# Softmax sums inverted to rows by VectorE blocks and GpSimd transfers, in place of TensorE transposes

## The chip, the core and the metric

The kernel runs on one core of a Trainium2 chip. TensorE multiplies matrices, VectorE and ScalarE work on tiles in SBUF and PSUM, GpSimd and SyncE issue transfers. What counts is the device time of one run, in microseconds (us).

## The reference

Three stages in one launch, on 4 batches of 576 positions, all in float32:

```python
q_rot, k_rot = (rotate(q), rotate(k))                # 4 batches, 8 heads, 576 positions, width 64
scores = scale * np.matmul(q_rot, k_rot.transpose(0, 1, 3, 2))
attn = np.exp(scores - np.max(scores, axis=-1, keepdims=True))
attn = attn / (np.sum(attn, axis=-1, keepdims=True) + 1e-09)
x = heads_side_by_side(np.matmul(attn, v))           # (4, 576, 512)

xn = (x - mu) / np.sqrt(var + 1e-06) * g_ln          # first MLP, 512 -> 2048 -> 512
x = x + np.maximum(xn @ w_ch1, 0.0) @ w_ch2

h = gelu(x @ w_in)                                   # gated MLP with a mix over the positions
u, v = (h[..., :512], h[..., 512:])
v_s = w_sg @ ((v - mu) / np.sqrt(var + 1e-06) * g_ln) + b_sg[:, None]
out = x + (u * v_s) @ w_out
```

## The kernel before

Everything is kept with the channels on the partitions and the positions along the columns. The batches are four groups, 0 to 3. In a group the attention is cut into eight blocks: four pairs of heads, each with a full block (`hi` 0, 384 queries) and a half block (`hi` 1, 192 queries). A block runs through these steps:

- `unit`: TensorE makes the scores of 128 queries and both heads (tiles S, L299); VectorE takes the negated maximum of a row (L327), ScalarE the exponential (L336), which also adds up each row's sum in `su`, with the queries on the partitions.
- `turn` and `evac`: TensorE transposes the exponentials in 64-wide pieces into the PSUM tile T (L371); ScalarE or VectorE copies them out (L395 to L406).
- `scale`: VectorE adds 1e-9, inverts (L421) and spreads the inverse over 64 columns for each head (`rb`, L425 to L429).
- `values`: TensorE multiplies by the values (PV, L454), then transposes `rb` (L465), so that the inverse lies along the columns. ScalarE copies PV to `x0` (L467); VectorE multiplies `x0` by the transposed inverse from PSUM (L473, L477). In all blocks but the four full ones of group 0, PV and the inverse are the two banks of the one PSUM tile T, which `turn` uses too, and T is given back after the multiplication. In the four early blocks both stand in banks of the MLP.

The first MLP follows a group by one: LayerNorm (`ln`, `rest`), then passes of `up` (L728 to L730) and `down` (L758 to L760) matmuls, three for each tile since values are split in a high and a low part. Their results leave PSUM over ScalarE and VectorE (L736, L738). The weights are split by `convert` (L58, L60, L62, L708, L710) during the first part of the run. The gated MLP of all batches closes the program.

The order on every engine is fixed when the program is built. `Sched` holds tasks as generators; each step names its engine, the earliest time and a planned duration, and the step that can start first on the planner's clock is written next, or one of lower rank that could start a little later. The ranks stand in tables (UNIT, RANK, TURN and others, by group). An engine then runs its own list strictly in that order, so a step that waits holds all that stands behind it on its engine. TensorE matmuls of `ones` (L562) fill planned gaps at the start. `x0` lives in a ring of XB = 9 tiles; the scores of a block wait until its tile is free.

Of the kernel before, what the change touches and what calls it, by code (L numbers as in the profile page):

```python
# [16 lines left out]
QB, KB, PB, TB, XB = 3, 4, 2, 2, 9  # L17
# [9 lines left out]
UNIT = [1.75, 2, 2.75, 4]  # L27
EVEN = [1, 0, 0, 3]
RANK = dict(end=-1, convert=2.75, prep=2.25, load=2, loader=2.75)
NORM, REST = [0.25, 2.75, 4.5, 2.5], [2.25, 2, 2.75, 4.5]  # L30
TURN, EVAC, VAL = [-1, 2.5, 3.5, 4], [1.5, 1.5, 1.5, 2.5], [2, 1.25, -1, 1.75]
# [116 lines left out]
class Attn:  # L148
# [10 lines left out]
    def __init__(self, tc, ctx, k, groups, sched):  # L159
# [6 lines left out]
        self.P, self.PT, self.QD = Bank(PB), Bank(TB), Bank(2)  # L166
        self.vin = [self.p.tile([128, 5, 128], F32, tag=f"vin{i}", name=f"vin{i}", bufs=1) for i in range(2)]
        self.qd = [self.p.tile([128, 128], F32, tag=f"qd{i}", name=f"qd{i}", bufs=1) for i in range(2)]
# [114 lines left out]
    def unit(self, i, heads=None):  # L283
# [18 lines left out]
        if heads[0] == 0:  # L302
            if u["t"] == 0:
                self.k["x0"](*x0)
                self.ahead(B["n"])
                B["su"] = self.p.tile([128, 6], F32, tag="su", name="su", bufs=3)
                B["left"] = 0
                B["turned"] = False
            u["P"], u["at"] = [], []
            u["nb"] = self.p.tile([128, 2], F32, tag="nb", name="nb", bufs=3)  # L310
# [103 lines left out]
    def scale(self, B, at):  # L414
# [7 lines left out]
        e = yield "DVE", 0.0, 0.4  # L422
        rb = B["rb"] = self.p.tile([128, 6, 64], F32, tag="rb", name="rb", bufs=2)
        if B["hi"]:
            nc.vector.tensor_copy(rb[:, 0:2, :], su[:, 0:2].unsqueeze(2).to_broadcast([128, 2, 64]))  # L425
            e = yield "DVE", 0.0, 0.2
            nc.vector.tensor_copy(rb[:, 2:4, :].rearrange("p a b -> p (a b)"), su[:, 2:3].to_broadcast([128, 128]))
        else:
            nc.vector.tensor_copy(rb, su.unsqueeze(2).to_broadcast([128, 6, 64]))  # L429
        B["inv"] = e + 0.1  # L430

    def values(self, B):
# [7 lines left out]
        for s, chs in enumerate(((0,), (1,), (2,), (3,), (4,)) if (B["g"], B["hi"]) in ALONE else ((0, 1, 2), (3, 4))):  # L440
            e = yield "PEc", (lambda: latest(B["ready"] if B["left"] == 0 else None, free(), V["v"])) if s == 0 else 0.0, 0.00168 * n * len(chs)
            self.pv = True
            if s == 0:
# [3 lines left out]
                else:  # L447
                    self.T.take()
                    both = self.ps.tile([128, 2, 512], F32, tag="T", name="PV")
                    ps, pb = both[:, 0, :], both[:, 1, :]  # L450
# [9 lines left out]
        f = yield "PE", lambda: latest(B.get("inv"), free() if early else 0.0), 0.08 + 0.00087 * n  # L460
        if early:
            bank2 = self.k["mpsb"].take()
            pb = self.k["mps"].tile([128, 512], F32, tag="m", name="inv")
        for i in range(3 if B["hi"] == 0 else 2):
            nc.tensor.transpose(pb[:, 128 * i:128 * i + 128], B["rb"][:, 2 * i:2 * i + 2, :].rearrange("p a b -> p (a b)"), self.k["ident"])  # L465
        e = yield "ACT", at + 0.35, 0.13 + 0.001 * n
        nc.scalar.copy(x0[:, q], ps[:, 0:n])  # L467
        if early:
            self.k["mpsb"].give(bank, e + 0.1)
        m = n if B["hi"] == 0 else 128  # L470
        e = yield "DVE", max(e, f + 0.25) + 0.1, 0.15 + 0.00105 * m
        a = q.start
        nc.vector.tensor_tensor(x0[:, a:a + m], x0[:, a:a + m], pb[:, 0:m], ALU.mult)  # L473
        for j in range(2) if B["hi"] else ():
            r = slice(64 * j, 64 * j + 64)
            e = yield "DVE", 0.0, 0.22
            nc.vector.tensor_tensor(x0[r, 512:576], x0[r, 512:576], pb[r, 128 + 64 * j:192 + 64 * j], ALU.mult)  # L477
        if early:
            self.k["mpsb"].give(bank2, e + 0.1)
        else:  # L480
            self.T.give(0, e + 0.1)
        n = B["ln"]
        self.rem[n] -= 1
        if self.rem[n] == 0:
            self.done[n] = e + 0.1
# [17 lines left out]
def fused_kernel(ctx, tc, q, k, v, cs, cst, w12, wi, wo, wsg, wsg4, gb, out):  # L503
# [39 lines left out]
    attn = Attn(tc, attn_ctx, dict(q=q, k=k, v=v, cs=csb, ident=ident, x0=get_x0, x0_free=x0_free, mps=mps, mpsb=mpsb), groups, C)  # L543
# [317 lines left out]
    for t in attn.qd:  # L861
# [341 lines left out]
```

## Time and profile before

| | |
|---|---|
| median of 3 runs | 932.64 us (931.2 to 932.87) |
| the profiled execution | 931.69 us, span 929.9 us |
| TensorE busy | 915.3 us, 98% of the span |
| VectorE, ScalarE busy | 600.4 us (65%), 495.2 us (53%) |
| GpSimd busy | 0.8 us, 9 instructions |
| mean granted TensorE clock | 0.998 |

The chain of work that ended last is 93% TensorE. Busy time of TensorE counts a pipelined matmul from its start to a modelled end, so what one costs is read from the start of one to the start of the next.

### The profile page before, as it was taken

How to read it: one execution, taken by the hardware profiler on the slowest of the kernel's cores; microseconds unless marked ns; L12 is line 12 of the kernel's file. 1: busy time of each engine (PE TensorE's matmuls, PEld its weight loads, DVE VectorE, ACT ScalarE, POOL GpSimd, SP SyncE). 2: the span in 40 equal slices, each digit the busy share in tenths (PEclk: the TensorE clock that was granted, in tenths of full speed). 3: DMA queues.
4: the chain of work that ended last, by engine and by line, in shares of the span. 5: the costliest groups of instructions: out<-in, count | busy, mean ns of one | idle time of the engine just before them, and what ended most of it. 6: DMA issues, size and time to landing. Idle time of an engine off the chain costs nothing.

```text
span 929.9 us, 18119 instructions
## 1 busy us (share of the span) xinstructions
PE 915.3 (98%) x7306; PEld 801.6 (86%) x7306; DVE 600.4 (65%) x1284; ACT 495.2 (53%) x1122; POOL 0.8 (0%) x9
## 2 busy tenths in 40 slices
PE   9998999999999999999999999999999999999998
PEld 9656778877988788779877799999999999999998
DVE  6868778888787645456764324663435897677654
ACT  3898888778365455463455513454313646373530
POOL 0000000000000000000000000000000000000000
PEclk9999999999999999999999999999999999999999
DMA  8366536676343363407633243988661201202011
GB/s 300 120 215 216 171 110 228 226 268 227 134 157 119 105 199 114 139 19 237 199 99 115 92 136 116 340 273 270 229 188 56 72 1 44 71 1 90 1 51 51
DMA packets 58067, 134.77 MB, mean 145 GB/s; under 512 B 8064, under 2 KB 30720, under 8 KB 57984
## 3 DMA queue, kind: packets, MB, share of 16 engines
q1 hardware_dynamic: 57152, 132.96, 43.2%
q8 instruction: 57, 0.93, 0.4%
q10 hardware_dynamic: 832, 0.66, 0.2%
q14 instruction: 26, 0.21, 0.1%
HBM read 106.50 MB, written 26.21 MB: 143 GB/s over the span
## 4 chain that ended last, share of the span: by engine, by line
PE 93%; DVE 3%; ACT 2%; issue 1%; POOL 0%; DVEq 0%; POOLq 0%
PE PV L454 9%; PE S L299 9%; PE m L758 8%; PE m L728 8%; PE m L759 7%; PE m L760 7%; PE m L730 7%; PE m L729 7%; PE T L371 5%; PE m L562 2%; PE p L1036 2%; PE p L1034 2%; PE p L1035 2%; PE p L1133 2%; PE p L1134 2%; PE p L1118 2%
## 5 line engine op out<-in xcount | busy, mean ns | idle before, releaser
L728 PE MATMUL m<-xh,w 128*128 128x288 f32 x480 | 148.0, 308 | 2.4 <-DVE h L738 2.4
L758 PE MATMUL m<-h,w 128*128 128x288 f32 x480 | 146.3, 305 | 0.0
L759 PE MATMUL m<-h,w 128*128 128x288 f32 x480 | 141.9, 296 | 0.0
L729 PE MATMUL m<-xl,w 128*128 128x288 f32 x480 | 141.6, 295 | 0.0
L730 PE MATMUL m<-xh,w 128*128 128x288 f32 x480 | 141.2, 294 | 0.0
L760 PE MATMUL m<-h,w 128*128 128x288 f32 x480 | 140.3, 292 | 0.0
L327 DVE TENSOR_REDUCE nb<-S 128x1 f32<-128x576 f32 x144 | 105.0, 753 | 35.0 <-PE S L299 30.5
L336 ACT ACTIVATE P<-S,nb 128x576 f32<-128x576 f32 x144 | 106.7, 744 | 36.1 <-DVE nb L327 35.3
L738 DVE SCALAR_TENSOR_TENSOR h<-m,h 128x288 fp32r<-128x288 f32 x128 | 58.3, 455 | 92.8 <-ACT h L736 91.5
L395 ACT COPY PT<-T 128x1024 f32<-128x1024 f32 (+6 forms) x118 | 75.0, 654 | 79.5 <-PE T L371 78.9
L736 ACT ACTIVATE h<-m 128x288 fp32r<-128x288 f32 x128 | 52.5, 410 | 92.5 <-PE m L730 91.1
L728 PEld LDWEIGHTS m<-xh,w 128*128 128x128 f32 x480 | 90.0, 187 | 9.4 <-DVE h L738 4.2
L299 PE MATMUL S<-K,qin 64*128 64x288 f32 x512 | 93.0, 430 | 1.7 <-ACT P L336 1.7
L758 PEld LDWEIGHTS m<-h,w 128*128 128x128 f32 x480 | 89.9, 187 | 5.4 <-issue 2.3
L759 PEld LDWEIGHTS m<-h,w 128*128 128x128 f32 x480 | 90.3, 188 | 0.5
L729 PEld LDWEIGHTS m<-xl,w 128*128 128x128 f32 x480 | 90.2, 188 | 0.6
L730 PEld LDWEIGHTS m<-xh,w 128*128 128x128 f32 x480 | 90.3, 188 | 0.0
L760 PEld LDWEIGHTS m<-h,w 128*128 128x128 f32 x480 | 90.2, 188 | 0.0
L454 PE MATMUL PV<-PT,vin 128*64 128x384 f32 (+1 forms) x640 | 87.3, 417 | 1.2 <-ACT PT L406 1.2
L371 PEld LDWEIGHTS T<-ident,P 64*128 64x128 f32 x1312 | 54.3, 138 | 29.3 <-DVE x L473 6.6
L454 PEld LDWEIGHTS PV<-PT,vin 128*64 128x64 f32 x640 | 43.8, 139 | 33.1 <-issue 27.2
L371 PE MATMUL T<-ident,P 64*128 64x64 f32 x1312 | 63.2, 227 | 4.7 <-DVE xc L587 1.9
(152 smaller groups left out, 1774.6 us busy)
## 6 DMA issues: line engine op xcount, KB each, us to landing
w<-wsc SPq DMA_DIRECT2D x96, 512.0 KB, 3.8
cd<-in_w SPq DMA_DIRECT2D x32, 512.0 KB, 4.5
wsc<-w SPq DMA_DIRECT2D x24, 512.0 KB, 3.6
kin<-in_k SPq DMA_DIRECT2D x15, 576.0 KB, 5.8
vin<-in_v SPq DMA_DIRECT2D x20, 320.0 KB, 3.7
qin<-in_q SPq DMA_DIRECT2D x15, 384.0 KB, 5.5
x1d<-x SPq DMA_DIRECT2D x32, 144.0 KB, 2.9
x<-x1d SPq DMA_DIRECT2D x32, 144.0 KB, 3.0
```

The source lines that it names most:

```text
L299: nc.tensor.matmul(S[j][:, n, :], q, Kb["K"][r, a:a + HQ], start=True, stop=True)
L327: nc.vector.tensor_reduce(nb[:, j:j + 1], S[j], AX.XY, ALU.max, negate=True)
L336: nc.scalar.activation(P[:, 576 * j:576 * j + 576].rearrange("p (n k) -> p n k", n=2), S[j], AF.Exp, bias=nb[:, j:j + 1], scale=1.0, accum ...
L371: nc.tensor.transpose(ps[:, j, 64 * n:64 * n + 64], x["tile"][r, 128 * i:128 * i + 128], self.k["ident"][r, r])
L395: copy(t[:, i:i + n, q0:q0 + 128].rearrange("p c (j q) -> p j c q", j=2), ps[:, :, 64 * s:64 * s + 64 * n].rearrange("p j (c q) -> p j c q ...
L454: nc.tensor.matmul(ps[r, 0:n], V["vin"][:, ch, r], t[:, 4 if ch == 4 else 5 * j + ch, 0:n], start=ch == 0, stop=ch == 4)
L728: nc.tensor.matmul(ps, w[:, 0, ms], xh[:, kc, :], start=kc == 0, stop=False)
L729: nc.tensor.matmul(ps, w[:, 0, ms], xl[:, kc, :], start=False, stop=False)
L730: nc.tensor.matmul(ps, w[:, 1, ms], xh[:, kc, :], start=False, stop=kc == 3)
L758: nc.tensor.matmul(ps, w[:, 0, ms], t[:, 0, :], start=a == 0, stop=False)
L759: nc.tensor.matmul(ps, w[:, 1, ms], t[:, 0, :], start=False, stop=False)
L760: nc.tensor.matmul(ps, w[:, 0, ms], t[:, 1, :], start=False, stop=a == n - 1)
```

## The change

In all blocks but the four full ones of group 0 (`ALONE`), the inverse sums no longer go through TensorE. `su` becomes a 128x32 tile that is set to zero once. VectorE transposes it in 32x32 blocks (`st`). GpSimd writes it with four small transfers to DRAM as rows of 128 queries (`inv`), and reads it back with two transfers (full block) or four (half block), each spread over 64 partitions, into `rb`, a 128x384 tile in SBUF. VectorE multiplies `x0` by `rb` in one instruction; T is given back after ScalarE's copy. `rb` has two buffers with a bank of their own in the planner (`R`). XB goes from 9 to 8, and all rank tables have other numbers, so that the order of the whole program is another one.

```diff
@@ -14,7 +14,7 @@
 DRAM = bass.MemoryType.DRAM
 
 HQ = 288
-QB, KB, PB, TB, XB = 3, 4, 2, 2, 9
+QB, KB, PB, TB, XB = 3, 4, 2, 2, 8
 WB, WX, CB = 8, 3, 4
 KC = (0, 288, 576)
 PARTS = (((0, 128), (128, 128), (256, 128)), ((384, 128), (512, 64)))
@@ -24,11 +24,11 @@
 HOLD = 0.3
 SWITCH = 0.3
 ALONE = ((0, 0),)
-UNIT = [1.75, 2, 2.75, 4]
...
-RANK = dict(end=-1, convert=2.75, prep=2.25, load=2, loader=2.75)
...
+UNIT = [1.75, 3, 1.75, 4]
...
+RANK = dict(end=0, convert=4.5, prep=4.5, load=4, loader=0.25)
...
 FG = [4, 8, 8, 4]
 
 AHEAD = 2
@@ -163,8 +163,9 @@
         self.S = [self.ps.tile([128, 2, 512], F32, tag=f"S{j}", name=f"S{j}")[:, :, 0:HQ] for j in range(2)]
         self.Sfree = [0.0, 0.0]
         self.T, self.qin, self.kin, self.vfree, self.K = Bank(), Bank(QB), Bank(2), Bank(2), Bank(KB)
-        self.P, self.PT, self.QD = Bank(PB), Bank(TB), Bank(2)
+        self.P, self.PT, self.QD, self.R = Bank(PB), Bank(TB), Bank(2), Bank(2)
         self.vin = [self.p.tile([128, 5, 128], F32, tag=f"vin{i}", name=f"vin{i}", bufs=1) for i in range(2)]
+        self.su = [self.p.tile([128, 32], F32, tag=f"su{i}", name=f"su{i}", bufs=1) for i in range(3)]
         self.qd = [self.p.tile([128, 128], F32, tag=f"qd{i}", name=f"qd{i}", bufs=1) for i in range(2)]
         self.done, self.rem, self.pv = {}, {}, False
         self.blocks, self.units = [], []
@@ -303,7 +304,7 @@
             if u["t"] == 0:
                 self.k["x0"](*x0)
                 self.ahead(B["n"])
-                B["su"] = self.p.tile([128, 6], F32, tag="su", name="su", bufs=3)
+                B["su"] = self.su[B["n"] % 3]
                 B["left"] = 0
                 B["turned"] = False
             u["P"], u["at"] = [], []
@@ -419,15 +420,33 @@
         nc.vector.tensor_scalar_add(su, su, 1e-9)
         e = yield "DVE", 0.0, 0.15
         nc.vector.reciprocal(su, su)
-        e = yield "DVE", 0.0, 0.4
-        rb = B["rb"] = self.p.tile([128, 6, 64], F32, tag="rb", name="rb", bufs=2)
-        if B["hi"]:
-            nc.vector.tensor_copy(rb[:, 0:2, :], su[:, 0:2].unsqueeze(2).to_broadcast([128, 2, 64]))
-            e = yield "DVE", 0.0, 0.2
-            nc.vector.tensor_copy(rb[:, 2:4, :].rearrange("p a b -> p (a b)"), su[:, 2:3].to_broadcast([128, 128]))
-        else:
-            nc.vector.tensor_copy(rb, su.unsqueeze(2).to_broadcast([128, 6, 64]))
-        B["inv"] = e + 0.1
+        if (B["g"], B["hi"]) in ALONE:
+            e = yield "DVE", self.R.free, 0.4
+            B["rslot"] = self.R.take()
+            rb = B["rb"] = self.p.tile([128, 384], F32, tag="rb", name="rb", bufs=2)
+            nc.vector.tensor_copy(rb.rearrange("p (a b) -> p a b", b=64), su.unsqueeze(2).to_broadcast([128, 6, 64]))
+            B["inv"] = e + 0.1
+            return
+        e = yield "DVE", 0.0, 0.2
+        st = self.p.tile([128, 32], F32, tag="st", name="st", bufs=2)
+        nc.vector.transpose(out=st, in_=B["su"])
+        D = self.k["dram"].tile([6, 128], F32, tag="inv", name="inv", bufs=4)
+        e = yield "POOL", e + 0.1, 4.4
+        for i in range(4):
+            nc.gpsimd.dma_start(out=D[0:k, 32 * i:32 * i + 32], in_=st[32 * i:32 * i + k])
+        for j in range(2):
+            e = yield "POOL", (lambda: latest(e + 3.0, self.R.free())) if j == 0 else 0.0, 2.2 if B["hi"] else 1.1
+            if j == 0:
+                B["rslot"] = self.R.take()
+                rb = B["rb"] = self.p.tile([128, 384], F32, tag="rb", name="rb", bufs=2)
+            r = slice(64 * j, 64 * j + 64)
+            if B["hi"]:
+                nc.gpsimd.dma_start(out=rb[r, 0:128], in_=D[j:j + 1].to_broadcast([64, 128]))
+                nc.gpsimd.dma_start(out=rb[r, 128:192], in_=D[2:3, r].to_broadcast([64, 64]))
+            else:
+                nc.gpsimd.dma_start(out=rb[r].rearrange("p (t q) -> p t q", q=128),
+                                    in_=D.rearrange("(t j) q -> j t q", j=2)[j:j + 1].to_broadcast([64, 3, 128]))
+        B["inv"] = e + 4.0
 
     def values(self, B):
 
@@ -447,7 +466,7 @@
                 else:
                     self.T.take()
                     both = self.ps.tile([128, 2, 512], F32, tag="T", name="PV")
-                    ps, pb = both[:, 0, :], both[:, 1, :]
+                    ps = both[:, 0, :]
             for ch in chs:
                 for j in range(2):
                     r = slice(64 * j, 64 * j + 64)
@@ -457,32 +476,34 @@
         if V["users"] == 0:
             self.vfree.give(V["vslot"], e)
         at = e
-        f = yield "PE", lambda: latest(B.get("inv"), free() if early else 0.0), 0.08 + 0.00087 * n
-        if early:
-            bank2 = self.k["mpsb"].take()
-            pb = self.k["mps"].tile([128, 512], F32, tag="m", name="inv")
-        for i in range(3 if B["hi"] == 0 else 2):
-            nc.tensor.transpose(pb[:, 128 * i:128 * i + 128], B["rb"][:, 2 * i:2 * i + 2, :].rearrange("p a b -> p (a b)"), self.k["ident"])
+        if not early:
+            e = yield "ACT", at + 0.35, 0.13 + 0.001 * n
+            nc.scalar.copy(x0[:, q], ps[:, 0:n])
+            self.T.give(0, e + 0.1)
+            e = yield "DVE", lambda: latest(e + 0.1, B.get("inv")), 0.15 + 0.00105 * n
+            nc.vector.tensor_tensor(x0[:, q], x0[:, q], B["rb"][:, 0:n], ALU.mult)
+            self.through(B, e + 0.1)
+            return
+        f = yield "PE", lambda: latest(B.get("inv"), free()), 0.08 + 0.00087 * n
+        bank2 = self.k["mpsb"].take()
+        pb = self.k["mps"].tile([128, 512], F32, tag="m", name="inv")
+        for i in range(3):
+            nc.tensor.transpose(pb[:, 128 * i:128 * i + 128], B["rb"][:, 128 * i:128 * i + 128], self.k["ident"])
         e = yield "ACT", at + 0.35, 0.13 + 0.001 * n
         nc.scalar.copy(x0[:, q], ps[:, 0:n])
-        if early:
-            self.k["mpsb"].give(bank, e + 0.1)
-        m = n if B["hi"] == 0 else 128
-        e = yield "DVE", max(e, f + 0.25) + 0.1, 0.15 + 0.00105 * m
-        a = q.start
-        nc.vector.tensor_tensor(x0[:, a:a + m], x0[:, a:a + m], pb[:, 0:m], ALU.mult)
-        for j in range(2) if B["hi"] else ():
-            r = slice(64 * j, 64 * j + 64)
-            e = yield "DVE", 0.0, 0.22
-            nc.vector.tensor_tensor(x0[r, 512:576], x0[r, 512:576], pb[r, 128 + 64 * j:192 + 64 * j], ALU.mult)
-        if early:
-            self.k["mpsb"].give(bank2, e + 0.1)
-        else:
-            self.T.give(0, e + 0.1)
+        self.k["mpsb"].give(bank, e + 0.1)
+        e = yield "DVE", max(e, f + 0.25) + 0.1, 0.15 + 0.00105 * n
+        nc.vector.tensor_tensor(x0[:, q], x0[:, q], pb[:, 0:n], ALU.mult)
+        self.k["mpsb"].give(bank2, e + 0.1)
+        self.through(B, e + 0.1)
+
+    def through(self, B, e):
+
+        self.R.give(B["rslot"], e)
         n = B["ln"]
         self.rem[n] -= 1
         if self.rem[n] == 0:
-            self.done[n] = e + 0.1
+            self.done[n] = e
 
     def ahead(self, n):
 
@@ -540,7 +561,7 @@
 
     mpsb = Bank(2)
     attn_ctx = ExitStack()
-    attn = Attn(tc, attn_ctx, dict(q=q, k=k, v=v, cs=csb, ident=ident, x0=get_x0, x0_free=x0_free, mps=mps, mpsb=mpsb), groups, C)
+    attn = Attn(tc, attn_ctx, dict(q=q, k=k, v=v, cs=csb, ident=ident, x0=get_x0, x0_free=x0_free, mps=mps, mpsb=mpsb, dram=dram), groups, C)
     cctx = ExitStack()
     cpool = cctx.enter_context(tc.tile_pool(name="conv", bufs=1, side="right"))
 
@@ -858,7 +879,7 @@
     nc.gpsimd.memset(ones, 1.0 / 512.0)
     nc.scalar.dma_start(out=ident, in_=cst)
     nc.scalar.dma_start(out=gbt, in_=gb)
-    for t in attn.qd:
+    for t in attn.qd + attn.su:
         nc.gpsimd.memset(t, 0.0)
     nc.gpsimd.memset(eps[:, 0:1], 1e-6)
     nc.gpsimd.memset(eps[:, 1:2], 4e-6)
```

On TensorE, this is the end of the full block of the second pair of heads in group 1. PV is the product with the values, S the next unit's scores, T the transposes, m the MLP. Before:

```order
L729 MATMUL m<-xl,wx 128x288
L730 MATMUL m<-xh,wx 128x288
L454 MATMUL PV<-PT,vin_82 64x384 x10
L465 MATMUL PV<-ident,rb 128x128 x3
L299 MATMUL S_79<-K,qd_84 128x288 x2
L371 MATMUL T<-ident,P 128x64 x16
L728 MATMUL m<-xh,wx 128x288
```

and now:

```order
L780 MATMUL m<-h,w 128x288
L781 MATMUL m<-h,w 128x288
L473 MATMUL PV<-PT,vin_81 64x384 x10
L300 MATMUL S_79<-K,qd_86 128x288 x2
L372 MATMUL T<-ident,P 128x64 x16
L779 MATMUL m<-h,w 128x288
```

The three transposes between PV and S are gone; the transposes into T stand as close behind PV as they did.

On TensorE, this is what stands between the first LayerNorm mean (ln<-x) of group 0 and the first MLP matmul. Before:

```order
L583 MATMUL ln<-x_584,ones 128x288
L299 MATMUL S_79<-K,qin 128x288
L299 MATMUL S_80<-K,qin 128x288
L299 MATMUL S_79<-K,qin 128x288
L299 MATMUL S_80<-K,qin 128x288
L371 MATMUL T<-ident,P 128x64 x12
L454 MATMUL PV<-PT,vin_81 64x192 x10
L299 MATMUL S_79<-K,qd_84 128x288 x2
L465 MATMUL PV<-ident,rb 128x128 x2
L728 MATMUL m<-xh,w 128x288
```

and now, from the second unit's scores behind that mean on:

```order
L372 MATMUL T<-ident,P 128x64 x28
L473 MATMUL PV<-PT,vin_82 64x192 x10
L300 MATMUL S_79<-K,qd_86 128x288 x2
L372 MATMUL T<-ident,P 128x64 x16
L645 MATMUL ln<-xc,ones 128x288 x4
L300 MATMUL S_79<-K,qin 128x288
L300 MATMUL S_80<-K,qin 128x288
L372 MATMUL T<-ident,P 128x64 x12
L300 MATMUL S_79<-K,qin 128x288
L300 MATMUL S_80<-K,qin 128x288
L749 MATMUL m<-xh,w 128x288
```

More of the attention, and the LayerNorm variance (ln<-xc), stand ahead of the first MLP matmul.

On VectorE, the sums of the half block that follows are inverted; x is the product of the block before, acc, h and K, qin, w are MLP, rotation and weights. Before:

```order
L419 TENSOR_SCALAR su<-su 128x3
L421 RECIPROCAL su<-su 128x3
L425 COPY rb<-su 128x128
L427 COPY rb<-su 128x128
L327 TENSOR_REDUCE nb<-S_79 128x1
L395 COPY PT<-T 128x128
```

and now, with the multiplication of the full block ahead of it:

```order
L759 SCALAR_TENSOR_TENSOR h<-m,h 128x288
L484 TENSOR_TENSOR x_1603<-x_1603,rb 128x384
L420 TENSOR_SCALAR su_85<-su_85 128x3
L422 RECIPROCAL su_85<-su_85 128x3
L432 STREAM_TRANSPOSE st<-su_85 128x32
L328 TENSOR_REDUCE nb<-S_79 128x1
L328 TENSOR_REDUCE nb<-S_80 128x1
```

The spreading copies are gone and one transpose stands in their place. In the whole list a block's multiplication stands 3 to 28 rows behind its transpose; the 3 is the last block of group 3.

## Rows read from the trace of the kernel before

**Rows 1.** The page: busy us of each engine, share of the span, instructions.

```profile
PE 915.3 (98%) x7306; PEld 801.6 (86%) x7306; DVE 600.4 (65%) x1284; ACT 495.2 (53%) x1122; POOL 0.8 (0%) x9
```

**Rows 2.** Windows: length, busy PE, PEld, DVE, ACT, POOL, granted clock, DMA share, GB/s.

```profile
12.00:80.10 68.10, 63.96 (x557) 42.45 (x555) 51.29 (x97) 54.99 (x120) 0.00 (x0) 0.97 0.58 195
80.10:240.00 159.90, 157.78 (x1410) 127.05 (x1409) 133.03 (x279) 127.29 (x282) 0.00 (x0) 1.00 0.61 208
```

**Rows 3.** Groups by line, inverse transposes: busy us, mean ns, idle before.

```profile
L465 PE MATMUL PV<-ident,rb 128*128 128x128 f32 x68 | 13.5, 294 | 0.0
```

**Rows 4.** Timeline of PE, a full block's end: start us, us, instruction.

```profile
159.34 0.30 PE L729 MATMUL m<-xl,wx 128*128 128x288 f32 x1
159.48 0.29 PE L730 MATMUL m<-xh,wx 128*128 128x288 f32 x1
159.70 3.45 PE L454 MATMUL PV<-PT,vin 128*64 128x384 f32 x20
163.08 0.55 PE L465 MATMUL PV<-ident,rb 128*128 128x128 f32 x3
163.46 1.14 PE L299 MATMUL S<-K,qd 128*128 128x288 f32 x4
164.78 0.71 PE L371 MATMUL T<-ident,P 64*128 64x64 f32 x16 [0.19 <-DVE x L473]
165.42 0.40 PE L728 MATMUL m<-xh,wx 128*128 128x288 f32 x1
165.66 0.29 PE L729 MATMUL m<-xl,wx 128*128 128x288 f32 x1
```

**Rows 5.** The same view, around a half block's end.

```profile
379.97 0.76 PE L299 MATMUL S<-K,qin 64*128 64x288 f32 x4
380.56 0.53 PE L371 MATMUL T<-ident,P 64*128 64x64 f32 x12
...
383.35 1.85 PE L454 MATMUL PV<-PT,vin 128*64 128x192 f32 x20
385.13 0.44 PE L465 MATMUL PV<-ident,rb 128*128 128x128 f32 x2
385.50 1.24 PE L299 MATMUL S<-K,qin 64*128 64x288 f32 x8
```

**Rows 6.** Timeline of ACT and DVE behind the full block of Rows 4.

```profile
163.66 0.48 ACT L467 COPY x<-PV 128x384 f32<-128x384 f32 x1 [1.61 <-PE PV L465]
...
164.17 0.56 DVE L473 TENSOR_TENSOR x<-x,PV 128x384 f32<-128x384 f32 x1 [0.86 <-ACT x L467]
```

**Rows 7.** Waits of PE: us in total, times, longest.

```profile
PE m L728 <- DVE h L738: 2.4, 4, 0.8
...
PE T L371 <- DVE x L473: 1.9, 10, 0.2
```

**Rows 8.** Groups by line on DVE: the spreading copies.

```profile
L429 DVE COPY rb<-su 128x384 f32<-128x384 f32 x16 | 5.8, 360 | 0.5
...
L425 DVE COPY rb<-su 128x128 f32<-128x128 f32 x16 | 3.6, 226 | 0.5
```

**Rows 9.** Groups by line on ACT from 12 to 80.1 us.

```profile
L336 ACT ACTIVATE P<-S,nb 128x576 f32<-128x576 f32 x29 | 21.5, 744 | 11.0 <-DVE nb L327 10.5 <-DVE su L419 0.2
...
L58 ACT ACTIVATE ce<-cd 128x512 f32<-128x512 f32 x8 | 5.5, 682 | 1.3 <-DVE w L710 1.3
L60 ACT ACTIVATE cd<-cd 128x512 int32<-128x512 uint32 x8 | 5.4, 676 | 0.0
L708 ACT CAST w<-ce 128x512 fp32r<-128x512 f32 x7 | 4.4, 625 | 0.0
```

**Rows 10.** DMA issues: count, KB each, median us to landing.

```profile
kin<-in_k SPq DMA_DIRECT2D x15, 576.0 KB, 5.8
...
rstd<-rstd SPq DMA_DIRECT2D x12, 72.0 KB, 2.0
```

**Rows 11.** Timeline of SP's queue: one issue.

```profile
279.74 0.56 SPq L235 DMA_DIRECT2D qin<-in_q  x1
```

More of the change, by code (lines that the diff above doesn't have):

```diff
@@ L26 @@
 ALONE = ((0, 0),)
-UNIT = [1.75, 2, 2.75, 4]
-EVEN = [1, 0, 0, 3]
-RANK = dict(end=-1, convert=2.75, prep=2.25, load=2, loader=2.75)
-NORM, REST = [0.25, 2.75, 4.5, 2.5], [2.25, 2, 2.75, 4.5]
-TURN, EVAC, VAL = [-1, 2.5, 3.5, 4], [1.5, 1.5, 1.5, 2.5], [2, 1.25, -1, 1.75]
+UNIT = [1.75, 3, 1.75, 4]
+EVEN = [0, 3, 1, 0]
+RANK = dict(end=0, convert=4.5, prep=4.5, load=4, loader=0.25)
+NORM, REST = [0.75, 3.5, 2.25, 3], [4, 1.75, 0.5, 1.25]
+TURN, EVAC, VAL = [1.75, 4, 2.25, 4.5], [0.75, 1.25, 0.75, 1.25], [2, 1.75, 1.25, -1]
 FG = [4, 8, 8, 4]
```

## The prediction

> **What bounds the kernel now.** I read the page first. TensorE is busy for 915 of 930 us, and no other engine over two thirds [rows 1]. So only what TensorE issues, or waits for, can move the end. VectorE and ScalarE count where TensorE waits for them, and in one stretch: up to the first MLP matmul at 80.1 us. There ScalarE is busy for 55 of 68 us, and TensorE has only attention to do [rows 2]. That stretch is bound by the attention's round over ScalarE and VectorE; all behind it by TensorE.
>
> Then I read TensorE's timeline, from the start of one group of matmuls to the start of the next, since busy time overstates short ones. The steps are regular, so a stall shows as a longer step. At the end of a full block [rows 4] PV starts at 159.70, the three inverse transposes at 163.08, the next scores at 163.46 and the transposes into T only at 164.78. Four score matmuls ahead of T take 0.59 us elsewhere (379.97 to 380.56, [rows 5]); here 1.32. The table of waits gives the cause: T waits for VectorE's multiplication 10 times [rows 7]. It counts only 0.2 us each, since it starts where the last matmul's modelled end is; the step shows 0.73.
>
> **The change part by part.** All against the profiled execution, 931.69 us; the median of the three runs lies 0.95 above.
>
> *The inverse transposes.* 68 leave TensorE [rows 3]: three in 12 full blocks, two in 16 half blocks. Three hold it for 0.38 us, start to next start [rows 4], two for 0.37 (385.13 to 385.50, [rows 5]). That makes 12 x 0.38 + 16 x 0.37 = 10.5 us at most. A group's cost is partly the step to the next kind of matmul, which PV pays too then: by busy time 68 take 13.5 us in 28 groups, of which the overlapping ends are no cost. I take 9, between 8 and 10.5.
>
> The Trainium skill ("TensorE: Matmul & The Clock Gate", Part 4) gives about 275 ns for a transpose in a kernel's stream; 68 of them would be an estimated 19 us. The trace has 0.38 us for three, start to start, so the measurement decides, and that larger gain is not in my sum.
>
> *T given back earlier.* Now ScalarE copies PV only when the inverse transposes behind it are done (wait on L465, [rows 6]): it starts at 163.66, VectorE's product at 164.17, T's next transposes at 164.78. Afterwards PV's last matmul ends at 159.70 + 3.45 = 163.15. The copy takes 0.48, so T is free at about 163.7. The scores start at 163.08 and T could follow at 163.67 in any case. So the step falls from 1.32 to about 0.62: 0.7 us at 10 places, 7 us. It needs ScalarE free at that moment; it was (1.61 us idle before the copy). If ScalarE is late by its next work, a cast of 0.6 us, most of it is lost: 2 to 8. What comes late next is the scores themselves, with 0.05 us of slack.
>
> *Fewer breaks.* By the order, the MLP's run of matmuls is broken 88 times from its first matmul to the gated MLP, before 100 times. The step out of the MLP is 0.22 us (159.48 to 159.70) against 0.14 inside it, the first matmul behind T takes 0.24 (165.42 to 165.66) [rows 4]. That is 0.2 us a break, and up to 0.4 with the step from attention into the MLP (T's 16 take 0.64 there); 12 breaks at 0.3 are 3.6 us.
>
> *The start.* More stands ahead of the first MLP matmul: 3 more exponentials, 4 more weight conversions, and the whole LayerNorm variance of the first half, with its table of roots. For ScalarE this is 4 x (0.68 + 0.68 + 0.62) + 3 x 0.94 (the exponential of 0.74 and the reading of its sum) + about 6 for the LayerNorm, less 5 for nine evacuations that VectorE gets: 12 us [rows 9]. The attention moved ahead of that point is 8.5 us for TensorE (one more half block's PV at 1.78 and ten pairs of score matmuls at 0.29, [rows 5]; 56 transposes at 0.04, [rows 4]; four variance matmuls, about 2) and is saved later. If ScalarE's work is the limit, the first MLP matmul comes at 92 and 3.5 us are lost. ScalarE has 13 us idle in the stretch, so the loss can be 0; if its idle share repeats, 12 x 68/55 = 15 gives 6.5. I take 3.5.
>
> *VectorE's work.* 44 spreading copies at 0.22 to 0.36 go, 28 small transposes come, three products become one in a half block [rows 8]. VectorE gains some 10 us, but is no bound: 0.
>
> *The new path.* Add, inverse and transpose, then four GpSimd issues, a landing, two or four issues, a landing; then VectorE multiplies, and holds whatever stands behind it (maxima for the next scores, evictions of the MLP) until the rows are there. The planner allows 13.7 us (full: 0.1 + 4.4 + 3.0 + 2 x 1.1 + 4.0) and 15.9 (half) and fills the gap with other work; the product lies late in the order for that. The trace shows no GpSimd transfer. From below: six or eight issues at SyncE's 0.56 [rows 11] and two landings at 2.0 make 7.4 and 8.5. From above by the slowest landing, 5.8 [rows 10]: 15.0 and 16.1, a hold of 1.3 and 0.2 us, 12 x 1.3 + 16 x 0.2 = 19 us. These transfers are a few KB, nearest to the 72 KB row of 2.0, so the rows are there in time; I take 1 us for all holds. A lower bound under 0 I exclude: this path only adds waits.
>
> The Trainium skill ("DMA: Bandwidth & Descriptors", Anatomy of one DMA) gives a fixed 2.0 us per GpSimd transfer, and in its latency table a first byte after 1 us. By these a half block's path is estimated at 8 + 4 = 12 us, under the 15.9 allowed, and the holds would be 0.
>
> XB 8 lets a group's scores start one tile later; TensorE has MLP work for that time: 0.
>
> Sum: -9 - 7 - 3.6 + 3.5 + 1 = -15 us. 931.7 - 15 = 916.7; for the median 917.5.
>
> **The rivals.**
>
> *The order gives it back, 926.* ScalarE is held by a conversion that waits for its load where the copy of PV stands (in the new order two casts and a conversion stand right ahead of it), so T's stall stays: the 7 us go. With 1 us less on the start: -9 - 3.6 + 4.5 + 1 = -7. For it: up to 240 us ScalarE is busy for 127 of 160 us [rows 2]. Against: 7 of the 11 places with T close behind PV lie in later, emptier stretches.
>
> *All terms at their better ends, 908.* -10.5 - 8 - 4.8 + 0 + 0 = -23.
>
> *The path is late, 950: slower.* The mechanism is the price of a GpSimd issue. With landings of 2.0, a full block's path passes the planner's 13.7 when an issue takes over 1.6 us, a half block's 15.9 when over 1.5. At 2 us an issue, VectorE is held 2.4 us in a full block and 4.2 in a half: 12 x 2.4 + 16 x 4.2 = 96 us. TensorE now waits for VectorE's evictions only 4 times [rows 7] and has two MLP banks of slack, under 1 us, so a third to a half of it arrives: 30 to 48, say +33 net of the gain, 950. From about 1.75 us an issue (some 35 us of holds, 15 of which reach TensorE) the gain is gone. For it: six to eight issues in a row on one engine, and nothing in the trace to bound one from above. Against: the issues have up to 28 rows of VectorE work to hide behind.
>
> The Trainium skill ("SBUF — State Buffer", Who interferes with whom) names a way to this: a transfer issued from GpSimd has its descriptors written by GpSimd's own cores, which share a pair of ports with VectorE and are locked out while VectorE copies at double speed. The trace agrees on the double speed: a spreading copy takes 360 ns for 384 columns and 226 for 128, 0.52 ns a column; the product of 384 columns takes 560 [rows 6]. But just these copies go (44 of 48). The page adds that instructions with two SBUF inputs block GpSimd's reads only; were issues to wait for each of them too, at VectorE's 83% busy and 0.3 us of mean rest, 8 x 0.25 = 2 us come on the path. Alone that stays inside the planner's time; on top of slow issues it does not, and for it the late path has 0.14 and not 0.1.
>
> **How the numbers follow.** The forecast (911 to 922) gets 0.58: its terms are read start to start, and -9 and -7 can hardly be hidden with TensorE at 98%. The order gives it back: 0.17. Better ends: 0.11. The late path: 0.14. A measurement of this kernel tells about 0.2%, 1.9 us, from no change. Faster: 0.58 + 0.11 + 0.16 = 0.85; of the second case 0.01 falls within 0.2%, and of the late path 0.01: 0.02; slower 0.13. The range 906 to 931 leaves out the late path and some of the better ends. The likeliest case's own range is 911 to 922.
>
> **What would show it.** Right: no matmul between PV and the next scores; the step from these scores to T about 0.6 us and no wait of T for VectorE's product; ScalarE's copy straight after PV; the first MLP matmul at 88 to 95 us; TensorE's idle time lower behind it. The path is in time if VectorE's idle time before its product is released by ScalarE or by nothing, not by GpSimd's transfers. Wrong: waits of several us of VectorE for `rb`, and MLP matmuls that wait for evictions behind them; a first MLP matmul beyond 97 us; or T still waiting, now for ScalarE's copy.

## The result and the profile after

The changed kernel takes 919.19 us (median of 4, 918.51 to 919.56), the kernel before 932.75 in the same session: ratio 0.9857, interval 0.9839 to 0.9874. Forecast: 917.5, between 906 and 931. The profiled execution has a span of 917.3 us, before 929.9. The sum came out; two of its parts did not, and they are the subject below.

The page's busy line, which answers to [rows 1], and the two windows of [rows 2]:

```profile
PE 904.4 (99%) x7232; PEld 798.1 (87%) x7232; DVE 589.1 (64%) x1233; ACT 493.7 (54%) x1125; POOL 107.0 (12%) x212
```

```profile
12.00:80.10 68.10, 65.06 (x582) 43.11 (x580) 60.76 (x115) 56.07 (x125) 4.96 (x10) 1.00 0.72 246
80.10:240.00 159.90, 157.04 (x1367) 129.35 (x1368) 117.76 (x239) 123.35 (x276) 41.51 (x79) 0.99 0.58 196
```

TensorE's busy time fell by 10.9 us, its idle time by 1.7 (14.6 to 12.9). VectorE does less, GpSimd has 107 us of work, and the end is still TensorE's.

TensorE's timeline at a full block's end, which answers to [rows 4], and ScalarE's copy and VectorE's product of the same block, which answer to [rows 6]:

```profile
153.53 0.29 PE L781 MATMUL m<-h,w 128*128 128x288 f32 x1
153.75 3.45 PE L473 MATMUL PV<-PT,vin 128*64 128x384 f32 x20
157.13 1.24 PE L300 MATMUL S<-K,qd 128*128 128x288 f32 x4
158.29 0.71 PE L372 MATMUL T<-ident,P 64*128 64x64 f32 x16
158.94 0.40 PE L749 MATMUL m<-xh,wx 128*128 128x288 f32 x1
```

```profile
157.24 0.48 ACT L481 COPY x<-PV 128x384 f32<-128x384 f32 x1 [0.89 <-PE PV L473]
```

```profile
161.65 0.55 DVE L484 TENSOR_TENSOR x<-x,rb 128x384 f32<-128x384 f32 x1
```

No matmul stands between PV and the scores. The copy starts straight behind PV and ends at 157.72, and T waits for nothing. Yet the step from the scores to T is 1.16 us, not 0.62. Adding up every step of TensorE from one start to the next, by the kind of matmul it begins with, over the whole trace (us, before to after): inverse transposes 10.6 to 2.2, MLP 432.2 to 427.9, everything else of the attention and LayerNorm 271.1 to 271.0, gated MLP 211.6 in both.

The new path: groups by line on GpSimd and VectorE (busy us, mean ns, idle before), then its DMA issues (KB, median us to landing), which answer to [rows 10, 11]:

```profile
L436 POOL DMA_DIRECT2D inv<-st x112 | 57.1, 516 | 337.2 <-DVE st L432 336.9
L444 POOL DMA_DIRECT2D rb<-inv x32 | 17.0, 532 | 55.8 <-DMA inv<-st 49.9 <-PE T L372 5.3
L447 POOL DMA_DIRECT2D rb<-inv x24 | 15.4, 643 | 41.2 <-DMA inv<-st 40.3
L484 DVE TENSOR_TENSOR x<-x,rb 128x192 f32<-128x192 f32 (+1 forms) x28 | 12.2, 436 | 5.3 <-DMA rb<-inv 5.2
L432 DVE STREAM_TRANSPOSE st<-su 128x32 f32<-128x32 f32 x28 | 5.9, 211 | 0.9
```

```profile
rb<-inv POOLq DMA_DIRECT2D x24, 96.0 KB, 3.2
inv<-st POOLq DMA_DIRECT2D x64, 0.4 KB, 3.3
inv<-st POOLq DMA_DIRECT2D x48, 0.8 KB, 3.6
rb<-inv POOLq DMA_DIRECT2D x32, 32.0 KB, 2.6
```

An issue costs 0.52 to 0.64 us, and VectorE idles for its rows for 5.2 us in all. The Trainium skill ("DMA: Bandwidth & Descriptors", Anatomy of one DMA) gives a fixed 2.0 us per GpSimd transfer; these land in 2.6 to 3.6 (medians), so the measurement decides. Against 2.0 that makes a path of two landings 1.9 (half block: 3.3 and 2.6) to 2.8 us longer (full block: 3.6 and 3.2).

### The profile page after: what moved, and what is told of

Same layout as the page of the kernel before. It is cut to its first block, busy times and chain, and to the rows that moved or that the text cites. A ratio compares the mean times of both kernels' runs of the same rounds, so it can differ in the third digit from the quotient of the medians.

```text
span 917.3 us, 18308 instructions
## 1 busy us (share of the span) xinstructions
PE 904.4 (99%) x7232; PEld 798.1 (87%) x7232; DVE 589.1 (64%) x1233; ACT 493.7 (54%) x1125; POOL 107.0 (12%) x212
## 4 chain that ended last, share of the span: by engine, by line
PE 95%; ACT 2%; DVE 2%; issue 0%; POOL 0%; ACTq 0%; POOLq 0%
PE S L300 10%; PE PV L473 9%; PE m L779 8%; PE m L749 8%; PE m L780 7%; PE m L781 7%; PE m L751 7%; PE m L750 7%; PE T L372 5%; PE m L583 2%; PE p L1057 2%; PE p L1055 2%; PE p L1056 2%; PE p L1154 2%; PE p L1155 2%; PE p L1138 2%
## 5 line engine op out<-in xcount | busy, mean ns | idle before, releaser
L759 DVE SCALAR_TENSOR_TENSOR h<-m,h 128x288 fp32r<-128x288 f32 x128 | 58.3, 455 | 91.8 <-ACT h L757 91.2
L396 ACT COPY PT<-T 128x1024 f32<-128x1024 f32 (+5 forms) x113 | 70.5, 645 | 81.4 <-PE T L372 81.1
L436 POOL DMA_DIRECT2D inv<-st x112 | 57.1, 516 | 337.2 <-DVE st L432 336.9
L372 PEld LDWEIGHTS T<-ident,P 64*128 64x128 f32 x1312 | 58.1, 138 | 24.7 <-issue 5.4
L300 PEld LDWEIGHTS S<-K,qin 64*128 64x128 f32 x512 | 50.8, 186 | 23.2 <-issue 7.8
```

Of the source, the lines that this page charges most:

```text
L300: nc.tensor.matmul(S[j][:, n, :], q, Kb["K"][r, a:a + HQ], start=True, stop=True)
L372: nc.tensor.transpose(ps[:, j, 64 * n:64 * n + 64], x["tile"][r, 128 * i:128 * i + 128], self.k["ident"][r, r])
L396: copy(t[:, i:i + n, q0:q0 + 128].rearrange("p c (j q) -> p j c q", j=2), ps[:, :, 64 * s:64 * s + 64 * n].rearrange("p j (c q) -> p j c q ...
```

## The experiments

The two halves of the change were run apart, then single terms. Ratios are to the kernel before on the same chip; a difference to after is that of two ratios, times 932.

**The order alone.** Only the numbers at the top, in the kernel before:

```
-QB, KB, PB, TB, XB = 3, 4, 2, 2, 9
+QB, KB, PB, TB, XB = 3, 4, 2, 2, 8
 (and UNIT, EVEN, RANK, NORM, REST, TURN, EVAC, VAL as after)
```

> The kernel before with nothing but the new numbers for the planner (XB 8, UNIT to VAL as after): the inverse rows still go over TensorE. Theory (the path brings the gain, the order little): the 68 transposes stay (10.6 us by steps), T is still given back behind VectorE's product; the order gives 95 breaks of the MLP's run where before has 100, 5 x 0.3 = 1.5 us less, and the later first MLP matmul costs about 2. So 933, between 930 and 936, and at most 3 us of the 13.5 are gained. Rival (the order brings the gain, the path only goes with it): at least 8 of the 13.5 us come with it, 925 or less.

Measured 935.22, ratio 1.0040 (1.0028 to 1.0052): slower by 3.4. The first MLP matmul comes at 91.2, the attention behind it takes 7.5 us less, the MLP 0.4 less. The theory's 933 (930 to 936) holds, the rival is out; by the prediction's own two terms for the order it would have been no slower than before.

**The path alone.** The same numbers the other way round, in the kernel after.

> The kernel after with the planner's old numbers (XB 9, UNIT to VAL as before): the new path alone. Theory: transposes -8.4 us (steps of TensorE, before against after), T's step behind PV back to 1.17 us, some -2.5, two breaks fewer (98) -0.6, first MLP matmul near 80 us as before, so no loss at the start: 921, between 919 and 925. Rival (the order brings it, or the old numbers place the product where its rows are late): 928 or more, with VectorE waiting for the rows for more than 15 us.

Measured 931.58, ratio 0.9994 (0.9981 to 1.0007): nothing gained that could be told from zero. Neither side had this: the time is the rival's, its waits for rows (over 15 us) are not there. The profiled execution, at full clock, took 926.17, and VectorE waited 11.6 us for rows, 9.61 of them at the last block, where TensorE had other work and no idle row. TensorE's idle rows of over 0.6 us from 90 to 130 us, where before has none:

```profile
117.78 1.47 PE L300 MATMUL S<-K,qin 64*128 64x288 f32 x4 [1.90 <-ACT P L337]
123.03 0.71 PE L372 MATMUL T<-ident,P 64*128 64x64 f32 x16 [0.96 <-DVE xc L608]
124.90 0.40 PE L372 MATMUL T<-ident,P 64*128 64x64 f32 x6 [1.17 <-ACT PT L396]
125.96 3.45 PE L473 MATMUL PV<-PT,vin 128*64 128x384 f32 x20 [0.66 <-DVE PT L396]
```

This is the LayerNorm of the first group's second half (mean at L604, xc at L608). Its last product stands at 117.96 and its mean at 119.18; in before they stand at 110.22 and 111.61. The product didn't wait for its rows here; it stands late in VectorE's list, since the planner counts on the path's full time. The old numbers leave TensorE too little else: between 114.1 and 133 us there is no MLP matmul, and the waits of the attention lie open, 4.7 us, of which the first 1.90 come ahead of the product. Its other executions took 4 to 8 us more, at a mean granted clock of 0.990 to 0.994; a second trace shows why.

> The kernel after with the planner's old numbers, run again for its trace. The profiled execution of the first run took 926.2 us at a mean granted clock of 1.000, the eleven others 930 to 934 at 0.990 to 0.994. Theory: 930 to 934 again, with one or two stretches at half the clock, 10 us or more in all, right behind the places where TensorE stood still in the first trace (72 to 75 us, 117 to 126 us), and the rest of the step sums as there. Rival: the clock stays and the difference lies elsewhere, in waits for the inverse rows (over 20 us of VectorE's time).

Measured 930.47. Windows of that trace (the column behind GpSimd's is the granted clock):

```profile
74.00:81.00 7.00, 5.78 (x44) 3.58 (x41) 4.58 (x10) 4.86 (x15) 2.09 (x4) 0.52 0.71 207
...
122.00:125.00 3.00, 3.00 (x7) 2.05 (x7) 0.00 (x0) 0.00 (x0) 2.03 (x4) 0.50 1.02 375
```

Ten us at the lower of the two levels (1.2 GHz), right behind the stalls at 72 and 117 us; in the first trace the same stretches show 1.00. At half the clock they cost at most five, and the two spans (924.4, 928.7) differ by 4.3. Waits for rows were 13.1 us: the rival's 20 is not there.

**T held longer.** Behind the copy, VectorE multiplies into the other half of the buffer:

```
 nc.scalar.copy(x0[:, q], ps[:, 0:n])
+nc.vector.tensor_tensor(both[:, 1, 0:n], x0[:, q], ps[:, 0:n], ALU.mult)
```

> The kernel after, in which T is held longer: behind ScalarE's copy of PV VectorE multiplies the copy with PV into the other half of the same PSUM buffer (an extra instruction of the size of the old product, whose result nobody reads), so T is given back behind VectorE as before, while the order of TensorE stays row for row. It undoes the early release of T alone. By the prediction's term, 0.7 us at 10 places, the time rises by 7 us to 926. By the step sums of the two traces T's stall in before was only 1.32 - 1.17 = 0.15 us at 11 places and 0.18 at some 5 more, so +2.5 us: 921.7, between 920 and 924. If T's release is worth nothing at all, 919.

Measured 920.88, ratio 0.9880 (0.9868 to 0.9893), 2 us over after: the small estimate. TensorE at the same block:

```profile
156.41 1.24 PE L300 MATMUL S<-K,qd 128*128 128x288 f32 x4
157.66 0.71 PE L372 MATMUL T<-ident,P 64*128 64x64 f32 x16
```

```profile
157.04 0.56 DVE L481 TENSOR_TENSOR PV<-x,PV 128x384 f32<-128x384 f32 x1 [1.53 <-ACT x L481]
```

The buffer is held 0.6 us longer, to 157.60; the step grows from 1.16 to 1.25, not to the 1.32 of before, since the copy no longer waits for inverse transposes. The scores cover the rest. The extra instruction also gives VectorE 12 us of work (28 of them), so the 2 us are not T's alone. The spans differ by 0.7 only, since the first MLP matmul comes 1.0 earlier in this trace (89.7); behind it 1.8 us are lost.

**A longer path.** Each round of writes three times:

```
-for i in range(4):
+for i in [0, 1, 2, 3] * 3:
```

> The kernel after with each of the four writes of the inverse rows issued three times: 8 more GpSimd issues a block at 0.52 us, 4.2 us more on the path; TensorE's order stays row for row. The step from the last read's issue to VectorE's product is 4.3 to 9.4 us now and a landing about 3.0, so the slack is 1.3 to 6.4 us; 4.2 us more make holds of 18 us in the full blocks and 7 in the half blocks beside the 5 there are: 30 us in all. Theory of the prediction (a third to a half of VectorE's holds arrives at TensorE): +8 to +12, 929. Rival (the order keeps the product late and two MLP banks hide it): under +2, 921 or less. If a landing also grows with the issues in the queue: more than 50 us of holds and over 935.

Measured 983.57, ratio 1.0564 (1.0537 to 1.0591). It was a larger dose than meant: a write of the second round waits until the first round's write to the same place has landed, as GpSimd's timeline shows.

```profile
128.67 2.07 POOL L436 DMA_DIRECT2D inv<-st  x4 [3.96 <-DVE st L432]
131.89 1.03 POOL L436 DMA_DIRECT2D inv<-st  x2 [1.14 <-DMA inv<-st]
133.37 3.07 POOL L436 DMA_DIRECT2D inv<-st  x6 [0.45 <-DMA inv<-st]
```

These waits are 66.4 us in 28 blocks, so the path grew by 4.2 + 2.4 = 6.6 us. VectorE's waits:

```profile
DVE x L484 <- DMA rb<-inv: 91.8, 22, 8.6
```

One of them, and TensorE behind it:

```profile
180.16 0.56 DVE L484 TENSOR_TENSOR x<-x,rb 128x384 f32<-128x384 f32 x1 [6.82 <-DMA rb<-inv]
```

```profile
182.81 2.83 PE L300 MATMUL S<-K,qin 64*128 64x288 f32 x7 [3.72 <-ACT P L337]
```

VectorE holds the maxima, ScalarE the exponentials, TensorE the scores. From 160 to 240 us the granted clock is 0.91, over the run 0.970 (after: 0.998); the MLP alone, whose work is unchanged, goes from 427.9 to 458.9 us by steps. 87 us of holds cost 66 by the ratios; the fall of the mean clock, 0.028 over 982.7 us, is worth up to 27 of them.

**A little longer, without that wait.** The extra round goes to a second DRAM tile, ahead of the one that counts:

```
-for i in range(4):
-    nc.gpsimd.dma_start(out=D[...], ...)
+for X, i in [(X, i) for X in (inv2, D) for i in range(4)]:
+    nc.gpsimd.dma_start(out=X[...], ...)
```

> The kernel after with four more GpSimd writes of each block's inverse rows ahead of the four that count, into a second DRAM tile that nobody reads, so that no write waits for another one's landing: 4 x 0.52 = 2.1 us more on each block's path, all other order as it is. In after VectorE is held by rows at 4 places for 5.2 us; these grow by 4 x 2.1, and two or three of the places with the least slack join: 15 us of holds. At the rate of the run with three rounds of writes (87 us more of holds, 64 us more of time, 0.7) +7 us: 926; at the prediction's rate (a third to a half) +4: 923. If a hold costs only once it is longer than the MLP banks' slack: 919 to 920. If the path bound every block: 28 x 2.1 = 59 us of holds, 950 or more.

Measured 921.50, ratio 0.9900 (0.9883 to 0.9918), 4 us by the ratios, 2.2 by the spans:

```profile
DVE x L484 <- DMA rb<-inv: 13.5, 7, 3.4
```

```profile
194.45 0.56 DVE L484 TENSOR_TENSOR x<-x,rb 128x384 f32<-128x384 f32 x1 [2.39 <-DMA rb<-inv]
```

```profile
224.54 0.56 DVE L484 TENSOR_TENSOR x<-x,rb 128x384 f32<-128x384 f32 x1 [2.97 <-DMA rb<-inv]
```

The holds grew nearly as expected (13.5 for 15). The half clock lasts from about 79.6 to 86.4 us, where after has it from 81.6 to 85, yet the first MLP matmul comes at 90.7 in both. The 2.2 us of the spans come behind it: TensorE's order is the same, and by start times it falls back by 1.1 us at the scores behind the first of these two holds (0.48 us in after) and by 1.1 at an MLP matmul behind the second (0.07 in after). For 8.2 us more of holds, 2.2 to 4 us are a rate of 0.3 to 0.5: here the prediction's rate holds. So 2.1 us more on the path cost 2.2 to 4 us; 6.6 more cost everything.

**The clock at the start.** In after TensorE stands twice for ScalarE's evictions ahead of the first MLP matmul, and then runs at half clock:

```profile
79.12 0.59 PE L372 MATMUL T<-ident,P 64*128 64x64 f32 x12 [1.11 <-ACT PT L396]
80.99 2.94 PE L473 MATMUL PV<-PT,vin 128*64 128x192 f32 x20 [1.28 <-ACT PT L407]
83.86 1.77 PE L300 MATMUL S<-K,qd 128*128 128x288 f32 x4
85.57 0.71 PE L372 MATMUL T<-ident,P 64*128 64x64 f32 x16
```

```profile
82.00:84.00 2.00, 2.00 (x15) 1.12 (x11) 0.00 (x1) 0.87 (x4) 0.00 (x0) 0.50 0.90 288
```

First all planned idle time was filled:

```
-if attn.pv or z - a < 0.25:
+if did[0] or z - a < 0.25:
```

> The kernel after, whose planner goes on filling TensorE's planned idle time with matmuls of ones until the first MLP matmul (after stops at the first PV): 47 more of them, all ahead of the first MLP matmul, the rest of TensorE's order as it is but for two neighbours. In after the granted clock is halved from 81.6 to 85.5 us behind idle stretches at 77 to 81 us, which costs 2 us. Theory (these idle stretches bring the half clock): the clock stays at 1.00 there, 917 us. Rival (the fill goes where TensorE isn't idle on the chip): 47 x 0.13 us (step of one in after) = up to 6 us later, 922 to 925, and the clock with it or not.

Measured 927.36, ratio 0.9961 (0.9944 to 0.9978). The rival, and more: one fill takes 0.215 us where the planner counts 0.11, and the fills wait for buffers (`PE m L583 <- ACT x L493`, 2.5 us); first MLP matmul at 98.9, the half clock moved to 58 to 61 us. Then nine matmuls in those two places alone:

```
+self.warm(B, 4)   # block 5, ahead of its second transposes
+self.warm(B, 5)   # block 5, ahead of PV
```

> The kernel after with nine matmuls of ones (64 x 128 by 128) that nobody reads, four and five of them at the two places where TensorE stands for ScalarE's evictions for 1.11 and 1.28 us ahead of the first MLP matmul (79.1 and 81.0 us); the rest of the order is as it is. In the run with 47 more of them one took 0.215 us (10.1 us for 47), so they fit: 0.86 and 1.07. Theory (the idle time there brings the half clock of 81.6 to 85.5 us, which costs half of 3.9 us): the clock stays at 1.00, -1.9, so 917.3. Rival 1 (what stands there is too little work for the clock, the half level only moves): 919. Rival 2 (they collide with what comes next): 920 or more.

Measured 917.88, ratio 0.9856 (0.9839 to 0.9872); since before was 0.8 us faster in that session than with after, both were run side by side.

> The kernel after again, unchanged, beside the next one on the same chip: 918.5 to 919.6, a mean granted clock of 0.996 to 0.998, with a stretch of some 4 us at half the clock near 82 us.

> The kernel after with the nine matmuls of ones in TensorE's two idle places, again. If the clock is what they save: 1.0 to 2.0 us under the unchanged kernel of the same call, with a mean granted clock of 0.999 or 1.000 in most executions. If the first run's 917.9 was only that chip's pace (before took 0.8 us less there than in the runs that after was first timed with): within 0.5 us of it.

Measured 918.41 (ratio 0.9861, 0.9845 to 0.9878) and 917.40 (0.9847, 0.9832 to 0.9861). The same places with the nine matmuls:

```profile
77.72 1.11 PE L512 MATMUL m<-ones 64*128 64x128 f32 x8
79.00 0.59 PE L372 MATMUL T<-ident,P 64*128 64x64 f32 x12 [0.16 <-ACT PT L396]
79.42 1.33 PE L512 MATMUL m<-ones 64*128 64x128 f32 x10
80.86 1.85 PE L473 MATMUL PV<-PT,vin 128*64 128x192 f32 x20
82.64 1.24 PE L300 MATMUL S<-K,qd 128*128 128x288 f32 x4
83.81 0.71 PE L372 MATMUL T<-ident,P 64*128 64x64 f32 x16
```

```profile
82.00:84.00 2.00, 2.00 (x20) 1.19 (x18) 0.46 (x2) 1.97 (x8) 0.00 (x0) 1.00 1.00 333
```

PV's step falls from 2.87 to 1.78, that of the scores from 1.71 to 1.17. The mean clock was 1.000 in all eight executions with the nine matmuls (0.996 to 0.998 in after's eight), so without the idle time the half clock doesn't come. With it, it comes most times, not always: the kernel with XB 9 (below) has the same two stalls, 1.11 and 1.28 us, and its trace shows 1.00 there.

That the clock brings the 1.0 us is not shown, and the traces speak against it. The first of VectorE's products by `rb`, with its wait for the rows, and the first MLP matmul, in the unchanged kernel, then with XB 9 (there with the window and TensorE's wait), then with the nine matmuls:

```profile
84.39 0.36 DVE L484 TENSOR_TENSOR x<-x,rb 128x192 f32<-128x192 f32 x1 [2.44 <-DMA rb<-inv]
```

```profile
90.08 0.40 PE L749 MATMUL m<-xh,w 128*128 128x288 f32 x1
```

```profile
82.00:84.00 2.00, 2.00 (x16) 1.20 (x14) 0.00 (x0) 1.96 (x7) 0.00 (x0) 1.00 1.08 378
```

```profile
84.38 0.36 DVE L484 TENSOR_TENSOR x<-x,rb 128x192 f32<-128x192 f32 x1 [2.41 <-DMA rb<-inv]
```

```profile
88.47 0.76 PE L300 MATMUL S<-K,qin 64*128 64x288 f32 x4 [1.73 <-ACT P L337]
89.06 0.54 PE L372 MATMUL T<-ident,P 64*128 64x64 f32 x12
89.43 0.71 PE L300 MATMUL S<-K,qin 64*128 64x288 f32 x4
90.07 0.40 PE L749 MATMUL m<-xh,w 128*128 128x288 f32 x1
```

```profile
83.55 0.36 DVE L484 TENSOR_TENSOR x<-x,rb 128x192 f32<-128x192 f32 x1 [1.66 <-DMA rb<-inv]
```

In each of them, and in after's first trace (85.03 and 90.73), the first MLP matmul stands 5.69 us behind that product (89.23 with the nine matmuls): VectorE's rotations and maximum, ScalarE's exponential and TensorE's last scores follow one on the other. At full clock TensorE only stands 1.73 us for the exponential instead (XB 9). So the half clock cost nothing there. In the two profiled executions the rows came 0.84 us earlier with the nine matmuls, and the span is 0.8 us shorter; between two traces of the unchanged kernel the same place differs by 0.65 us. Whether the nine matmuls have a part in the earlier rows is open. The medians are 1.0 us apart, with intervals that overlap; 917.40 is the lowest of all versions run.

**All blocks on the path.** The first part too, with numbers of its own (the transposes of L491 are gone; the copy gives PV's bank back):

```
-if (B["g"], B["hi"]) in ALONE:  (spreading copy, return)
-if not early:
+(mpsb if early else T).give(...)
```

> The kernel after with the first part's four blocks on the new path too (no inverse transposes left on TensorE), and the planner's numbers chosen anew for that. The 12 transposes take 2.2 us of TensorE's steps in after; 92 breaks instead of 88 are 4 x 0.3 = 1.2 us more, and less attention stands ahead of the first MLP matmul. Theory: 918, between 914 and 922. Rival: the first LayerNorm, which has nothing but attention to hide behind, waits for the path of its fourth block, 11 us or more: the first MLP matmul later than 93 us and over 923.

Measured 921.24, ratio 0.9886 (0.9872 to 0.9900): inside the range, no gain. The 2.2 us of transposes are gone and the first MLP matmul comes at 85.5, so the rival is out; but the MLP's steps take 2.6 us more with 92 breaks, and the clock is at 0.57 from 78 to 86 us.

**XB.**

```
-QB, KB, PB, TB, XB = 3, 4, 2, 2, 8
+QB, KB, PB, TB, XB = 3, 4, 2, 2, 9
```

> The kernel after with XB 9 as before, the one number of the change that has no test yet. The planner's order differs by it: 90 breaks of the MLP's run, in after 88. Theory (a ninth tile does nothing by itself, as the prediction had it): 2 breaks at 0.4 us (TensorE's MLP steps are 4.3 us shorter in after than in before, by 12 breaks), 920, between 918.5 and 922. Rival (the eighth tile's wait costs something in after, which a ninth gives back): 917 or less.

Measured 921.52, ratio 0.9890 (0.9876 to 0.9905): inside the range, though its MLP steps took 2.8 us more for two breaks. The tile can't be told from the order that goes with it.

## Why the prediction was right, and where it was not

*The inverse transposes, -9.* Measured -8.4 by steps (10.6 to 2.2, what is left being the first part's 12); all 68 of [rows 3] are gone. Right.

*T given back earlier, -7.* This term failed, in the step "four score matmuls ahead of T take 0.59 us elsewhere". That row [rows 5] is of `qin` scores on 64 rows, 0.76 us busy; behind a full block's PV stand the next half block's `qd` scores on 128 rows, 1.14 us busy, in the very lines of [rows 4]. They need 1.16 by themselves. Only 0.16 of the 1.32 was a stall, at 11 places, and 0.18 at five with eight scores (1.25 to 1.07): 11 x 0.16 + 5 x 0.18 = 2.7 us. Holding T again cost 2. The 0.2 us a place that the waits gave [rows 7] was the better number, and the prediction argued it away.

*Fewer breaks, -3.6.* 88, as said; TensorE's MLP steps are 4.3 us shorter. Over six orders they went with the breaks, not evenly: 427.9 at 88, 430.7 at 90, 430.5 at 92, 431.8 at 95, 432.5 at 98, 432.2 at 100.

*The start, +3.5.* First MLP matmul at 90.7 (88 to 95 said), 10.6 later for 8.5 us of work moved (the prediction's four parts add up to 8.9): about +2. What ends the stretch is not ScalarE's work, as said, but the first block's rows: VectorE waits 3.03 us for them, and the first MLP matmul follows that product by 5.7 us in six traces.

*Holds, +1.* 5.2 us of VectorE's time at 4 places; TensorE's waits for VectorE's evictions go from 2.4 to 2.8 us. The 3.03 us of them at the start are counted there: with T held longer the first product came 1.95 us earlier (83.08) and the first MLP matmul 1.0 (89.7). So the size is right, the place was not seen. The reads are not a few KB, as said, but 16 to 96 KB, and all landings take longer than the 2.0 that the sum went by.

Together -8.4 - 2.7 - 4.3 + 2 = -13.4, with the other holds under 0.5; the spans say -12.6, the medians -13.6. That the forecast came so near is partly luck: the T term was 4.3 too large while breaks, start and holds came out about 3 better. The rival that the order gives T's term back did not happen by its mechanism: ScalarE copies straight behind PV (0.05 us, in 27 of 28 blocks).

What the sum hid is that its terms were added as if independent. By them the path alone is worth 15 us and the order nothing. Run apart, the order costs 3.4, the path gives 0.2 (5.5 in one execution at full clock), and only both give 13.6. With either order a product follows its block's small transpose by 10 to 17 us. With the old one a LayerNorm comes 7.6 us later for it (119.18 against 111.61) while TensorE has no MLP work left, and 4.7 us of stalls with the half clock behind them take most of the gain back. Why the order alone costs 3.4 is settled only in part: the first MLP matmul comes 11 us later and 7.5 come back; the inverse transposes take 13.2 us by steps there (10.6 in before), among them 1.28 us in which the first LayerNorm waits for VectorE's product. Of the 16.0 us of span between the order alone and after, these transposes are 10.9, the MLP's steps 3.9 (95 breaks to 88).

*The late path, 950.* It did not come: an issue costs 0.52 to 0.64 us, not the 1.75 that would lose the gain. Its price for a hold, a third to a half, held at 8 us more of holds (0.3 to 0.5) and was too low at 87 more (0.76), in part since long stalls take the clock with them. The gain's loss, put at 35 us of holds (its own terms make 46 at 1.75 us an issue: 12 x 0.9 + 16 x 2.2), lies between 13.5 (9 of the 13 us left) and 91.8 (66 us lost).

## What to carry to other kernels

Before a step is called a stall, subtract the step of the same instruction in the same form (operands, rows), not of its line. When work goes from a busy engine to a long path, its price is the order's to hide: time the path with the old order and the order with the old path before either gets the credit. Long waits of TensorE are to be priced with the clock that follows them; a short fall of the clock costs something only where nothing later waits anyway, so follow the chain to the next fixed point before it gets a price.

## What the runs showed of the hardware

Four score matmuls (as the timeline counts them) of 288 columns take 0.59 us from start to start on 64 rows and 1.16 on 128. A granted clock of 0.5 (1.2 GHz) for 3.4 or 6.8 us followed stalls of TensorE that came to 2 to 4 us, none of them over 1.9 us long, in before, after, the path alone and the version with all blocks on the path; such stalls left it at 1.00 in one execution of the path alone and in the trace with XB 9, and why is open. GpSimd's issues stayed at 0.50 to 0.66 us beside a VectorE that was 74 to 89% busy up to 240 us. GpSimd's small transfers landed in 2.6 to 3.6 us (medians); the first block's rows came up to 2 us earlier or later from one execution to the next with TensorE's order the same (first product at 83.1 to 85.0).
